# The seven-product feed-forward: p kept in the bank of h, new engine orders, a second tile in eight products, weight sums on VectorE

## The chip, the cores and the metric

One core of a Trainium2 chip runs the whole program. The metric is device time in microseconds (us) of one execution; lower is better. The kernel before takes 4196.09 us (median of 3 runs, 4193.67 to 4196.6).

## The reference, cut to what matters

Three stages follow each other on 24576 tokens of 256 numbers: a filter in the frequency domain, a mixture of experts, and a dense feed-forward. The change is in the last one alone:

```python
def _moe2_ref(x, w_in, w_out):      # x 3072*8 x 256, w_in 256 x 2048, w_out 2048 x 256
    h = x @ w_in
    g = h - np.tanh(h)
    return (g @ w_out).astype(np.float32)
```

The kernel is for small h. There g is h times a polynomial of third degree in u = h*h, written as g = (s + KAPPA) * p with p = c*h*u and s = (u + beta)^2.

## The kernel before

The first two stages fill the first 1776 us and are not touched. The feed-forward (`ff_phase`, line 1035) goes over 48 tiles of 512 tokens. The x of a tile (256 x 512) is cut into 2 x 2 blocks, and so is `w_in`; h of a tile then comes from seven block products in place of eight (Winograd's form of Strassen's scheme), with sums of the blocks of x and of the weights in place of the eighth. Every fp32 number is held as a high and a low part, so one block product M1 to M7 is three matmuls of 256 columns (`product`, line 1123). A tile has eight groups j; group g = 8*tile + j is 128 columns of each half of h, in two PSUM banks `B[0]` and `B[1]` (line 1061), with two pairs of banks that alternate between even and odd groups.

For each group the engines do this, by the names of the order tables:

- TensorE (PE): M5 and M1 into `B[0]`, then M6, M7, M2, M3, M4; and D0 to D7, the product with `w_out` of the group three before (`down`, line 1166): for each quarter of the tokens and each half f a matmul of 512 columns with the high part gh and one of 256 with the low part gl.
- ScalarE (ACT): `op1` copies half a bank of `B[0]` to `B[1]`, `opa` copies the other half to SBUF as A; `u0`, `u1` square the two banks; `s` squares again; `gh` rounds g to its high part.
- VectorE (DVE): `opb`, `opc` add A into the banks in place (line 1211); `p0`, `p1` make p from h and u, 128 x 512 each (line 1219); `g` makes (s + KAPPA) * p, 128 x 1024 in one instruction (line 1224).
- GpSimd (POOL): `gl` = g - gh, 128 x 1024 (line 1231).

Per tile there are also: the load of x and of the row numbers two tiles ahead (`ld`); four block subtractions on x (`ta` and `tb`, two each); their high parts on ScalarE (`ha`, `hb`, `hc`) and low parts on GpSimd (`la`, `lb`, `lc`); four sums of the finished output on VectorE (`sum0` to `sum3`, line 1173), and four indirect DMAs that scatter the rows to the output, issued by GpSimd (`row0` to `row3`, line 1177).

The order of work on each engine is written in two tables, `FIRST` for tile 0 and `LATER` for the others, one string for each group (lines 1005 to 1022). `SHIFT` says which group a name belongs to (D is three groups late, M5 and M1 one early), and `NEEDS` what must have been emitted before it. The engines run their lists in order and wait on each other by semaphores. Buffers set further waits: `p` has two buffers, so `p0` of a group waits for `gl` of the group two before; a bank of h is free for the group two later when `p0` and `p1` have read it.

Tile 0 is done in eight products (`plain`, line 1108: six matmuls of 512 columns for each half and group), since the sums of weight blocks `Sh` and `Sl` do not exist yet. They are made beside tile 0: `whole` adds high and low parts of `w_in` on GpSimd (line 1143), `sums_of` and `Sl` run on VectorE, `Sh` on ScalarE. Near the end `column_sums` (tile 45), `column_max` (tile 46) and `limit` (tile 47) work out a bound on h; a branch to a slow path behind it is not taken.

Of the kernel before, what the change touches and what calls it, by code (L numbers as in the profile page):

```python
# [988 lines left out]
def ff_first(tc, pool, x2T, ids, c):  # L989
# [43 lines left out]


def ff_phase(tc, x2T, ids, out, weights, mx, N, X0):
# [5 lines left out]
    with ExitStack() as es:  # L1041
# [89 lines left out]
        def sums_of(c):  # L1131
            w = slice(TH * c, TH * c + TH)
            v = nc.vector
            v.tensor_tensor(R[:, 0], F[:, 0, 1], F[:, 1, 1], op=ALU.add)
            v.tensor_tensor(R[:, 1], R[:, 0], F[:, 0, 0], op=ALU.subtract)
            v.tensor_tensor(R[:, 2], F[:, 0, 0], F[:, 0, 1], op=ALU.subtract)
            v.tensor_tensor(R[:, 3], F[:, 1, 0], R[:, 1], op=ALU.subtract)

        def whole(c):
            w = slice(TH * c, TH * c + TH)  # L1140
            a, b = [q.bitcast(F32).rearrange("p k (f n) -> p k f n", f=2) for q in (wih, wil)]
            for k in range(2):
                nc.gpsimd.tensor_tensor(F[:, k], a[:, k, :, w], b[:, k, :, w], op=ALU.add)  # L1143
# [42 lines left out]
        def emit(n, g):  # L1186
            t, j = divmod(g, 8)
            f = n[-1:].isdigit() and int(n[-1])
            if n[0] == "M":
# [22 lines left out]
            elif n[0] == "u":  # L1212
                if f == 0:
                    U[g] = tp.tile([128, 2, TM], F32, name="u")
                nc.scalar.activation(U[g][:, f], B[f][g % 2], AF.Square)  # L1215
            elif n[0] == "p":
                if f == 0:
                    Q[g] = tp.tile([128, 2, TM], F32, name="p")
                nc.vector.scalar_tensor_tensor(Q[g][:, f], B[f][g % 2], Q3[2], U[g][:, f], op0=ALU.mult, op1=ALU.mult)  # L1219
# [3 lines left out]
            elif n == "g":  # L1223
                nc.vector.scalar_tensor_tensor(Q[g], O.pop(g), KAPPA, Q[g], op0=ALU.add, op1=ALU.mult)  # L1224
                U.pop(g)
            elif n == "gh":
                G[g] = [tp.tile([128, 2, TM], F32R, name=n, bufs=3)]
                nc.scalar.activation(G[g][0], Q[g], AF.Copy)  # L1228
            elif n == "gl":
                G[g].append(tp.tile([128, 2, TM], F32R, name=n, bufs=3))  # L1230
                nc.gpsimd.tensor_tensor(G[g][1], Q.pop(g), G[g][0].bitcast(F32), op=ALU.subtract)  # L1231

        def extra(n, t):
            f = n[-1:].isdigit() and int(n[-1])
# [30 lines left out]
        def place(k, n):  # L1265
            t = k // 8
            if n in TILE:
                g = t + TILE[n]
                return (n, g) if 0 <= g < NT and (t or n[:2] not in ("su", "ro")) else None
            if n[0] in "FS":  # L1270
                return (n, 0) if t < 2 else None
            g = k + SHIFT.get(n, 0)
            return (n, g) if 0 <= g < NG and not (g < 8 and n in STEPS) else None
# [128 lines left out]
```

## Time and profile before

| | before |
|---|---|
| median of 3 runs | 4196.09 us |
| the profiled execution | 4197.41 us |
| its span in the trace | 4195.6 us |
| mean granted TensorE clock | 0.961 of full speed |
| PE busy, share of the span | 93% |
| VectorE, ScalarE, GpSimd busy | 68%, 61%, 59% |
| start of the feed-forward's first matmul | 1776.35 us |

The profiled execution is 1.3 us longer than the median, and 1.8 us of it lie outside the span. Busy time of PE overlaps: a matmul is shown to its modelled end, while the next one starts earlier, so the distance between starts tells the rate. All times below are us from the start of the span.

### The profile page before, as it was taken

The page shows a single profiled execution, that of the slowest core. Times are in us where ns is not written, and L with a number is a line of the kernel's source. Part 1 is how long each engine was busy: PE and PEld are TensorE (multiplying, and loading weights), DVE is VectorE, ACT ScalarE, POOL GpSimd, SP SyncE. Part 2 cuts the span into 40 slices and gives each one's busy share as a digit, 9 for nine tenths or more (in the row PEclk, how much of TensorE's full clock was granted, in tenths as well). Part 3 has the DMA queues.
Part 4 walks back from the last instruction along what each step waited for, and adds up shares of the span by engine and source line. Part 5 has one row for each costly group of instructions (what it writes and reads, how often), then busy time and mean ns, then how long its engine had stood idle before and what let it go on. Part 6 is the DMA issues. An engine that isn't in the chain of part 4 may idle for free.

```text
span 4195.6 us, 67878 instructions
## 1 busy us (share of the span) xinstructions
PE 3888.7 (93%) x23932; PEld 3499.4 (83%) x23932; DVE 2871.2 (68%) x4727; ACT 2556.9 (61%) x4396; POOL 2488.4 (59%) x1609
## 2 busy tenths in 40 slices
PE   6999899999999999979999998999999989999988
PEld 3666679999999999968888888888888888888877
DVE  4788866888888777666666656666666665666666
ACT  3666564555555555556666666666666666666665
POOL 2476664544444444466666666666666666666655
PEclk8999999999999999999999999999999999999999
DMA  8999863222332232100000000000000000000000
GB/s 260 285 293 292 252 174 105 62 80 77 79 79 57 76 77 70 53 16 21 21 26 21 22 25 21 21 21 21 21 26 21 26 21 21 21 21 21 26 16 16
DMA packets 296660, 300.39 MB, mean 72 GB/s; under 512 B 157041, under 2 KB 238970, under 8 KB 296314
## 3 DMA queue, kind: packets, MB, share of 16 engines
q1 hardware_dynamic: 233466, 191.28, 17.0%
q10 hardware_dynamic: 44416, 53.77, 3.9%
q0 software_dynamic: 18432, 50.95, 3.4%
q8 instruction: 190, 3.11, 0.3%
q14 instruction: 156, 1.28, 0.1%
HBM read 278.98 MB, written 132.24 MB: 98 GB/s over the span
## 4 chain that ended last, share of the span: by engine, by line
PE 31%; issue 11%; POOL 9%; DVE 5%; DMA 1%; ACT 1%; POOLq 0%; DVEq 0%
PE h L1129 16%; PE po L1168 10%; PE po L1169 5%; POOL out L1177 4%; POOL gl L1231 3%; POOL xl L1263 2%; DVE p L1224 2%; DVE h L1211 1%; DMA out<-ob,ix 1%; DVE ob L1173 1%; DVE p L1219 0%; ACT gh L1228 0%; POOL work L1143 0%; POOLq L1177 0%; ACT abs L1074 0%
## 5 line engine op out<-in xcount | busy, mean ns | idle before, releaser
L1231 POOL TENSOR_TENSOR gl<-p,gh 128x1024 fp32r<-128x1024 f32 x384 | 917.9, 2397 | 761.7 <-ACT gh L1228 586.8
L1168 PE MATMUL po<-wo,gh 128*128 128x512 f32 x3072 | 1156.3, 401 | 0.5 <-ACT gh L1228 0.5
L1169 PE MATMUL po<-wo,gl 128*128 128x256 f32 x3072 | 882.0, 287 | 136.6 <-POOL gl L1231 136.6
L1219 DVE SCALAR_TENSOR_TENSOR p<-h,u 128x512 f32<-128x512 f32 x768 | 525.3, 684 | 435.3 <-POOL gl L1231 250.2
L1215 ACT ACTIVATE u<-h 128x512 f32<-128x512 f32 x768 | 458.2, 597 | 513.0 <-PE h L1129 508.2
L1169 PEld LDWEIGHTS po<-wo,gl 128*128 128x128 f32 x3072 | 591.9, 193 | 153.6 <-POOL gl L1231 153.1
L1168 PEld LDWEIGHTS po<-wo,gh 128*128 128x128 f32 x3072 | 593.5, 193 | 75.0 <-ACT gh L1228 0.8
L1211 DVE TENSOR_TENSOR h<-h,A 128x256 f32<-128x256 f32 x752 | 322.8, 429 | 423.9 <-PE h L1129 407.7
L1224 DVE SCALAR_TENSOR_TENSOR p<-s,p 128x1024 f32<-128x1024 f32 x384 | 573.9, 1494 | 17.0 <-ACT s L1222 15.2
L822 POOL TENSOR_TENSOR w2l<-raw,w2h 128x1024 fp32r<-128x1024 f32 x126 | 339.2, 2693 | 392.5 <-ACT w2h L821 390.2
L1129 PE MATMUL h<-xh,Sh 128*128 128x256 f32 x1504 | 469.2, 312 | 78.0 <-DVE h L1211 71.7
L884 ACT ACTIVATE hh<-h 128x384 fp32r<-128x384 f32 (+1 forms) x548 | 266.4, 499 | 430.3 <-PE h L874 430.0
L1222 ACT ACTIVATE s<-u,beta 128x1024 f32<-128x1024 f32 x384 | 442.9, 1153 | 12.5
L1129 PEld LDWEIGHTS h<-xh,Sh 128*128 128x128 f32 x1504 | 301.2, 200 | 170.4 <-DVE h L1211 110.7
L1129 PE MATMUL h<-xl,Sh 128*128 128x256 f32 x1504 | 439.7, 292 | 0.0
L1129 PE MATMUL h<-xh,Sl 128*128 128x256 f32 x1504 | 439.1, 292 | 0.0
L1228 ACT ACTIVATE gh<-p 128x1024 fp32r<-128x1024 f32 x384 | 407.4, 1061 | 51.1 <-DVE p L1224 49.0
L874 PE MATMUL h<-yh,w1h 128*128 128x384 f32 (+1 forms) x1184 | 391.7, 331 | 14.9 <-DVE hl L885 11.2
L874 PE MATMUL h<-yh,w1l 128*128 128x384 f32 (+1 forms) x1184 | 387.7, 327 | 0.6 <-DVE w1l L822 0.5
L874 PE MATMUL h<-yl,w1h 128*128 128x384 f32 (+1 forms) x1184 | 387.4, 327 | 0.0
L902 PE MATMUL o<-hh,w2h 128*128 128x384 f32 (+1 forms) x1184 | 387.1, 327 | 0.0
L902 PE MATMUL o<-hh,w2l 128*128 128x384 f32 (+1 forms) x1184 | 387.0, 327 | 0.0
(243 smaller groups left out, 9062.2 us busy)
## 6 DMA issues: line engine op xcount, KB each, us to landing
raw<-in_w SPq DMA_DIRECT2D x256, 512.0 KB
y<-region SPq DMA_DIRECT2D x252, 99.0 KB
xt<-in_x SPq DMA_DIRECT2D x48, 512.0 KB
z1d<-a ACTq DMA_DIRECT2D x96, 256.0 KB
A<-z1d SPq DMA_DIRECT2D x64, 384.0 KB
z3d<-b ACTq DMA_DIRECT2D x128, 192.0 KB
bt<-z3d SPq DMA_DIRECT2D x96, 256.0 KB
x2T<-x SPq DMA_DIRECT2D x63, 384.0 KB
```

Of the source, the lines that this page charges most:

```text
L874: nc.tensor.matmul(h[j], p[:, k, c], q[:, k], start=n == 0, stop=n == 5)
L902: nc.tensor.matmul(O[v][d], p[:, fb, c], q[:, j], start=fb == 0 and n == 0 and (d == 0 or v >= KV), stop=fb == 7 and n == 2 and (d == 1 or ...
L1129: nc.tensor.matmul(h, a[:, w], b, start=n == "M5" and a is ah and b is xh, stop=False, skip_group_check=True)
L1168: nc.tensor.matmul(po, gh[:, c], flat(wo[:, f]), start=begin, stop=False)
L1169: nc.tensor.matmul(po[:, :D], gl[:, c], wo[:, f, 0], start=False, stop=end)
L1211: nc.vector.tensor_tensor(B[n == "opc"][g % 2][:, first], B[1][g % 2][:, second], A5[g % 2], op=ALU.add)
L1215: nc.scalar.activation(U[g][:, f], B[f][g % 2], AF.Square)
L1219: nc.vector.scalar_tensor_tensor(Q[g][:, f], B[f][g % 2], Q3[2], U[g][:, f], op0=ALU.mult, op1=ALU.mult)
L1222: nc.scalar.activation(O[g], U[g], AF.Square, bias=beta)
L1224: nc.vector.scalar_tensor_tensor(Q[g], O.pop(g), KAPPA, Q[g], op0=ALU.add, op1=ALU.mult)
L1228: nc.scalar.activation(G[g][0], Q[g], AF.Copy)
L1231: nc.gpsimd.tensor_tensor(G[g][1], Q.pop(g), G[g][0].bitcast(F32), op=ALU.subtract)
```

## The change

- **p in the bank.** `p0` and `p1` write over h in its own PSUM bank. `g` is split in `g0` and `g1`, 128 x 512 each, which read s from SBUF and p from the bank. The two-buffer tile `p` is gone; g has two buffers of its own, needed only from `g0` on. A bank is now free for the group two later when `g0` (first bank) and `g1` (second bank) are done, where it was free after `p0` and `p1`.
- **New orders.** The tables `FIRST`, `SECOND` and `LATER` hold one list for a whole tile. The scatters stand apart and late, the four subtractions on x are single names `t1` to `t4`.
- **Two tiles in eight products.** `CLASSIC = 2`: tiles 0 and 1 use `plain`; tile 1's blocks of x get their parts by `cx` (ScalarE) and `cl` (GpSimd).
- **Weight sums on VectorE.** The adds of `whole` move from GpSimd (eight of 128 x 512) to VectorE (four of 128 x 1024), and the sums are spread over tiles 0 and 1.
- `column_sums` is emitted behind `s` of four groups of tile 45, and `limit` behind `g1` of the second group of tile 47.

```diff
 FIRST = dict(
...
+SECOND = dict(
...
 LATER = dict(
...
-    POOL=("ta gl", "tb gl", "la gl", "gl row0 row1 row2 row3 lb", "lc gl ld", "gl", "gl", "gl"),
+    POOL=("gl gl t3 t1 t2 gl la gl t4 gl gl lc lb ld gl row2 gl row1 row0 row3"),
 )
...
+    M5=("lb", "g0-2"), M1=("M5", "la"), M6=("op1", "lb"), M7=("opb", "lc"), M3=("opb", "la"), M2=("opb", "opa", "la", "g0-2"), M4=("opc", "lc", "g1-2"),
...
+CLASSIC = 2
...
-                if t:
+                if t >= CLASSIC:
...
             elif n[0] == "u":
-                if f == 0:
+                if g not in U:
                     U[g] = tp.tile([128, 2, TM], F32, name="u")
                 nc.scalar.activation(U[g][:, f], B[f][g % 2], AF.Square)
             elif n[0] == "p":
-                if f == 0:
-                    Q[g] = tp.tile([128, 2, TM], F32, name="p")
-                nc.vector.scalar_tensor_tensor(Q[g][:, f], B[f][g % 2], Q3[2], U[g][:, f], op0=ALU.mult, op1=ALU.mult)
+                h = B[f][g % 2]
+                nc.vector.scalar_tensor_tensor(h, h, Q3[2], U[g][:, f], op0=ALU.mult, op1=ALU.mult)
             elif n == "s":
                 O[g] = tp.tile([128, 2, TM], F32, name="s", bufs=1)
                 nc.scalar.activation(O[g], U[g], AF.Square, bias=beta)
-            elif n == "g":
-                nc.vector.scalar_tensor_tensor(Q[g], O.pop(g), KAPPA, Q[g], op0=ALU.add, op1=ALU.mult)
-                U.pop(g)
+                U.pop(g - 1, None)
+                if t == NT - 3 and j > 3:
+                    column_sums(j - 4)
+            elif n in ("g0", "g1"):
+                if f == 0:
+                    Q[g] = tp.tile([128, 2, TM], F32, name="g")
+                nc.vector.scalar_tensor_tensor(Q[g][:, f], O[g][:, f], KAPPA, B[f][g % 2], op0=ALU.add, op1=ALU.mult)
+                if (t, n, j) == (NT - 1, "g1", 1):
+                    limit()
...
             elif n[0] == "F":
-                whole(f)
+                a, b = [q.bitcast(F32).rearrange("p k (f n) -> p k f n", f=2) for q in (wih, wil)]
+                nc.vector.tensor_tensor(F, a[:, :, :, c], b[:, :, :, c], op=ALU.add)
...
```

The order of instructions shows what the tables do. First, GpSimd over one steady tile before: x<-x are the subtractions, xl the low parts, out the row scatters.

```order
L1251 TENSOR_TENSOR x<-x 128x256
L1252 TENSOR_TENSOR x<-x 128x256
L1231 TENSOR_TENSOR gl<-p,gh 128x1024
L1254 TENSOR_TENSOR x<-x 128x256
L1255 TENSOR_TENSOR x<-x 128x256
L1231 TENSOR_TENSOR gl<-p,gh 128x1024
L1263 TENSOR_TENSOR xl<-x,xh 128x768
L1231 TENSOR_TENSOR gl<-p,gh 128x1024 x2
L1177 DMA out<-ob,ix 24576x256 x4
L1263 TENSOR_TENSOR xl<-x,xh 128x512 x2
L1231 TENSOR_TENSOR gl<-p,gh 128x1024 x4
```

And the same engine over one steady tile of the changed kernel:

```order
L1237 TENSOR_TENSOR gl<-g,gh 128x1024 x2
L1264 TENSOR_TENSOR x<-x 128x256 x3
L1237 TENSOR_TENSOR gl<-g,gh 128x1024
L1275 TENSOR_TENSOR xl<-x,xh 128x768
L1237 TENSOR_TENSOR gl<-g,gh 128x1024
L1264 TENSOR_TENSOR x<-x 128x256
L1237 TENSOR_TENSOR gl<-g,gh 128x1024 x2
L1275 TENSOR_TENSOR xl<-x,xh 128x512 x2
L1237 TENSOR_TENSOR gl<-g,gh 128x1024
L1178 DMA out<-ob,ix 24576x256
L1237 TENSOR_TENSOR gl<-g,gh 128x1024
L1178 DMA out<-ob,ix 24576x256 x3
```

The four scatters and two low parts that stood in one run between the third and the fourth gl are now three runs: two low parts, one scatter, three scatters.

Second, VectorE where group 1 of a steady tile ends and group 2 begins, before. h_20430 and h_20432 are the two banks of even groups, h_20431 and h_20433 those of odd ones.

```order
L1219 SCALAR_TENSOR_TENSOR p<-h_20431,u 128x512
L1211 TENSOR_TENSOR h_20430<-h_20432,A_25157 128x256
L1219 SCALAR_TENSOR_TENSOR p<-h_20433,u 128x512
L1211 TENSOR_TENSOR h_20432<-h_20432,A_25157 128x256
L1173 TENSOR_REDUCE ob<-po 128x256
L1224 SCALAR_TENSOR_TENSOR p<-s,p 128x1024
```

And in the changed kernel:

```order
L1219 SCALAR_TENSOR_TENSOR h_20431<-h_20431,u 128x512
L1212 TENSOR_TENSOR h_20430<-h_20432,A_24506 128x256
L1219 SCALAR_TENSOR_TENSOR h_20433<-h_20433,u 128x512
L1212 TENSOR_TENSOR h_20432<-h_20432,A_24506 128x256
L1229 SCALAR_TENSOR_TENSOR g<-s,h_20431 128x512
L1229 SCALAR_TENSOR_TENSOR g<-s,h_20433 128x512
L1174 TENSOR_REDUCE ob<-po 128x256
```

p goes back to the banks h_20431 and h_20433, the two halves of g read them there, and the output sum stands behind g.

Third, VectorE in tile 45, where the column sums are added (l<-abs,abs), before:

```order
L1219 SCALAR_TENSOR_TENSOR p<-h_20431,u 128x512
L1075 TENSOR_TENSOR l_20437<-abs_42011,abs_42012 128x512
L1211 TENSOR_TENSOR h_20430<-h_20432,A_41978 128x256
L1219 SCALAR_TENSOR_TENSOR p<-h_20433,u 128x512
L1211 TENSOR_TENSOR h_20432<-h_20432,A_41978 128x256
```

And in the changed kernel:

```order
L1229 SCALAR_TENSOR_TENSOR g<-s,h_20433 128x512
L1090 TENSOR_TENSOR l_20437<-abs_42287,abs_42288 128x512
L1219 SCALAR_TENSOR_TENSOR h_20432<-h_20432,u 128x512
L1219 SCALAR_TENSOR_TENSOR h_20430<-h_20430,u 128x512
L1212 TENSOR_TENSOR h_20431<-h_20433,A_42283 128x256
```

In both, the add stands ahead of the add into a bank (opb) that the next block products wait for.

## Rows read from the trace of the kernel before

**Rows 1.** Windows: stretch, us, busy of PE PEld DVE ACT POOL, PEclk, DMA, GB/s
```profile
1776.00:1830.00 54.00, 40.48 (x185) 32.02 (x184) 37.46 (x40) 29.21 (x39) 34.26 (x21) 0.97 0.10 27
1830.00:1886.00 56.00, 47.75 (x297) 43.08 (x296) 36.08 (x49) 33.85 (x55) 35.30 (x21) 0.90 0.07 19
1886.00:4017.00 2131.00, 1958.83 (x12734) 1783.49 (x12733) 1310.71 (x1892) 1397.92 (x2194) 1423.61 (x818) 0.95 0.08 22
4017.00:4079.00 62.00, 50.19 (x301) 45.42 (x300) 38.65 (x50) 37.03 (x61) 35.31 (x22) 0.89 0.06 18
4079.00:4177.00 98.00, 88.44 (x593) 79.39 (x592) 69.92 (x108) 63.24 (x98) 53.75 (x30) 1.00 0.03 12
```

**Rows 2.** Timeline of PE without waits: start, duration, engine, line, operation
```profile
2802.34 0.39 PE L1168 MATMUL po<-wo,gh 128*128 128x512 f32 x1
...
2803.39 0.28 PE L1129 MATMUL h<-xh,Sh 128*128 128x256 f32 x1
...
2805.15 0.40 PE L1168 MATMUL po<-wo,gh 128*128 128x512 f32 x1
```

**Rows 3.** Timeline of PE, same tile, at D0 of group 3
```profile
2812.97 0.40 PE L1168 MATMUL po<-wo,gh 128*128 128x512 f32 x1
2816.29 0.39 PE L1169 MATMUL po<-wo,gl 128*128 128x256 f32 x1 [2.92 <-POOL gl L1231]
...
2818.16 0.41 PE L1129 MATMUL h<-xh,wih 128*128 128x256 f32 x1
...
2820.48 0.28 PE L1129 MATMUL h<-xh,Sl 128*128 128x256 f32 x1
```

**Rows 4.** Timeline of POOL, same tile, from gl of group 2 on
```profile
2802.51 2.40 POOL L1231 TENSOR_TENSOR gl<-p,gh 128x1024 fp32r<-128x1024 f32 x1 [3.24 <-issue]
2805.07 2.00 POOL L1177 DMA_INDIRECT out<-ob,ix  x1 [0.16 <-issue]
...
2811.37 2.57 POOL L1263 TENSOR_TENSOR xl<-x,xh 128x512 fp32r<-128x512 f32 x2
2813.86 4.69 POOL L1231 TENSOR_TENSOR gl<-p,gh 128x1024 fp32r<-128x1024 f32 x2
```

**Rows 5.** Waits, tiles 2 to 44: who for whom, us in total, times, longest
```profile
DVE p L1219 <- POOL gl L1231: 241.2, 42, 5.8
...
PE po L1169 <- POOL gl L1231: 123.6, 43, 2.9
...
PE h L1129 <- DVE h L1211: 48.6, 129, 1.6
```

**Rows 6.** Groups of instructions, tiles 2 to 44: busy us, mean ns of one
```profile
L1231 POOL TENSOR_TENSOR gl<-p,gh 128x1024 fp32r<-128x1024 f32 x345 | 823.5, 2393 | 659.6 <-ACT gh L1228 505.0 <-issue 140.9 <-PE h L1129 13.7
...
L1224 DVE SCALAR_TENSOR_TENSOR p<-s,p 128x1024 f32<-128x1024 f32 x344 | 513.4, 1492 | 12.2 <-ACT s L1222 10.5
L1219 DVE SCALAR_TENSOR_TENSOR p<-h,u 128x512 f32<-128x512 f32 x688 | 470.8, 684 | 401.1 <-POOL gl L1231 241.2 <-ACT u L1215 158.5
...
L1215 ACT ACTIVATE u<-h 128x512 f32<-128x512 f32 x689 | 411.3, 597 | 467.2 <-PE h L1129 462.9
...
L1222 ACT ACTIVATE s<-u,beta 128x1024 f32<-128x1024 f32 x344 | 396.8, 1153 | 11.2
L1228 ACT ACTIVATE gh<-p 128x1024 fp32r<-128x1024 f32 x344 | 364.9, 1061 | 37.1 <-DVE p L1224 35.1
...
L1211 DVE TENSOR_TENSOR h<-h,A 128x256 f32<-128x256 f32 x688 | 295.4, 429 | 394.9 <-PE h L1129 379.8 <-ACT u L1215 2.3 <-issue 0.3
```

**Rows 7.** Timeline of VectorE and POOL, one g beside one xl
```profile
2842.42 2.14 DVE L1224 SCALAR_TENSOR_TENSOR p<-s,p 128x1024 f32<-128x1024 f32 x1
...
2841.64 1.84 POOL L1263 TENSOR_TENSOR xl<-x,xh 128x768 fp32r<-128x768 f32 x1
```

**Rows 8.** Lines 1224 and 1075: ns min/median/max of one instruction
```profile
L1224 DVE SCALAR_TENSOR_TENSOR p<-s,p x384: 1207/1216/6597, 1781.1 to 4177.3; 128x1024 f32<-128x1024 f32 x192
...
L1075 DVE TENSOR_TENSOR l<-abs,abs x4: 1910/1968/3493, 4040.2 to 4069.5; 128x512 fp32r<-128x512 f32 x4
```

More of the change, by code (lines that the diff above doesn't have):

```diff
@@ L1022 @@
+    POOL=("gl gl t3 t1 t2 gl la gl t4 gl gl lc lb ld gl row2 gl row1 row0 row3"),
 )
 STEPS = ("M1", "M3", "M5", "M6", "M7", "op1", "opa", "opb", "opc")
-TILE = dict(ta=1, tb=1, ha=1, hb=1, hc=1, la=1, lb=1, lc=1, ld=2, **{f"{n}{i}": -1 for n in ("sum", "row") for i in range(4)})
-SHIFT = dict(**{f"D{i}": -3 for i in range(8)}, M5=1, M1=1, op1=1, opa=1, u1=-1, s=-1, p1=-1, g=-1, gh=-1, gl=-1)
+TILE = dict(**{n: 1 for n in "t1 t2 t3 t4 ha hb hc la lb lc cx cl".split()}, ld=2, **{f"{n}{i}": -1 for n in ("sum", "row") for i in range(4)})
@@ L1026 @@
+SHIFT = dict(**{f"D{i}": -3 for i in range(8)}, M5=1, M1=1, op1=1, opa=1, u1=-1, s=-1, p1=-1, g0=-1, g1=-1, gh=-1, gl=-1)
 NEEDS = dict(
-    M5=("lb", "p0-2"), M1=("M5", "la", "p0-2"), M6=("op1", "lb"), M7=("opb", "lc"), M3=("opb", "la"), M2=("opb", "opa", "la"), M4=("opc", "M7", "lc", "p1-2"),
-    op1=("M1", "p1-2"), opa=("M1", "opb-2", "opc-2"), opb=("M6", "opa"), opc=("M7", "opa"), u0=("M2", "M3", "p1-2", "s-2"), u1=("M4", "u0"),
-    s=("u0", "u1", "g-1"), p0=("u0", "gl-2", "gh-2"), p1=("u1", "p0"), g=("s", "p0", "p1"), gh=("g", "D7-3"), gl=("gh", "D7-3"),
@@ new lines @@
+    op1=("M1", "g1-2"), opa=("M1", "opb-2", "opc-2"), opb=("M6", "opa"), opc=("M7", "opb"), u0=("M2", "M3", "p1-2", "s-2"), u1=("M4", "p1-2", "s-2"),
+    s=("u0", "u1", "g0-1", "g1-1"), p0=("u0",), p1=("u1",), g0=("s", "p0", "gl-2"), g1=("p1", "g0"), gh=("g0", "g1", "D7-3"), gl=("gh", "D7-3"),
+    **{f"D{i}": ("gl",) for i in range(8)}, **{f"row{i}": (f"sum{i}",) for i in range(4)},
+    **{f"{n}{i}": (f"{m}{i}",) for n, m in (("Sa", "F"), ("Sb", "Sa"), ("Sh", "Sb"), ("Sl", "Sh")) for i in range(4)},
@@ L1035, in ff_phase @@
+    **{f"F{i}": (f"Sb{i - 1}",) for i in range(1, 4)},
+    t1=("ld",), t2=("t1",), t3=("ld",), t4=("t2", "t3"), ha=("ld",), hb=("t1", "t2"), hc=("t3", "t4"), la=("ha",), lb=("hb",), lc=("hc",),
+    cx=("ld",), cl=("cx",))
+CLASSIC = 2
 def ff_phase(tc, x2T, ids, out, weights, mx, N, X0):
@@ L1129, in product @@
                 nc.tensor.matmul(h, a[:, w], b, start=n == "M5" and a is ah and b is xh, stop=False, skip_group_check=True)
[L1131 to L1143, printed above, removed]
         def general(h):
@@ L1263, in extra @@
                     nc.gpsimd.tensor_tensor(xl, v, xh.bitcast(F32), op=ALU.subtract)
[L1265 to L1273, printed above, removed]
+        once = lambda n: n in TILE or n[0] in "FS"
+        exists = lambda n, g: 0 <= g < (NT if n in TILE else NG) and not (g < 8 * CLASSIC and n in STEPS)
         def ready(n, g):
```

95 lines of the change are left out of this document (53 added, 42 removed), and 6 rows, old and new, of the table PE.

## The prediction

> **What bounds the kernel now.** I read the windows by stretch first: tile 0 to 1830, tile 1 to 1886, tiles 2 to 44 to 4017, tile 45 to 4079, tiles 46 and 47 to 4177. Tiles 2 to 44 take 2131 us and hold 12734 matmuls of PE [rows 1]. A tile issues 8 x (7 x 3 + 8 x 2) = 296 matmuls, so the stretch is 43.0 tiles of 49.5 us. No engine is full there: VectorE 1311, ScalarE 1398, GpSimd 1424 of 2131 us, and the clock is 0.95 on average.
>
> The timeline of PE says what a tile would take without waits. From 2802.34 to 2803.39 lie three D steps, 0.35 us each; from there to 2805.15 fifteen matmuls of 256 columns, 0.1173 us each [rows 2]. One product is then 0.352 us, a group 7 x 0.352 + 8 x 0.35 = 5.26 us, a tile 42.1 us. So 7.4 us of each tile are lost, 320 us over 43 tiles. Nearly all the stake of this change is there.
>
> Where they are lost is one place. At D0 of group 3 PE waits for gl [rows 3], 43 times in 43 tiles, 123.6 us in all, 2.9 us each [rows 5]. Behind it the clock is at its lower level, 1.2 GHz: a matmul shown with 0.28 us elsewhere has 0.41 at 2818.16, and 0.28 again at 2820.48 [rows 2, 3]. In tiles 46 and 47, where the clock reads 1.00 throughout [rows 1], nothing of this remains. From 2812.97 to 2820.48 PE issues what costs 2.0 us undisturbed (two D steps and eleven matmuls); it took 7.5, so 5.5 of the 7.4 us hang on this wait. The other 1.9 us are short waits for VectorE's adds into the banks (129 waits, 48.6 us as PE shows them [rows 5]) and the rest of the slow stretch.
>
> Why gl is late is in GpSimd's timeline [rows 4]. Behind gl of group 2 come four scatters and two xl, from 2805.07 to 2813.86, 8.8 us in one run (the scatters 6.3, so 1.58 each with the gap behind it). Only then gl of group 3 starts. The wait goes back further: p has two buffers, so VectorE's p0 stood up to 5.8 us behind gl, 42 times [rows 5], and with it all that follows in VectorE's list.
>
> **The change, part by part.**
>
> *The scatters.* The longest run of foreign work between two gl is now three scatters, 3 x 1.58 = 4.7 us, then two xl (2.57) and three subtractions. From the end of M4 of a group to the end of its gl the rows give u 0.60, s 1.15, two halves of g 1.37, gh 1.06, gl 2.39 [rows 6], together 6.6, with five handoffs of 0.1 to 0.2 us (0.16 between two GpSimd instructions [rows 4]) 7.2 us. In the new PE order 33 to 39 steps lie between M4 of a group and its D0, 11.6 to 13.7 us. So a gl may stand 4.4 us behind other work on the average place, and the three scatters stand at group 7, which has 12.6 us and bears 5.4. Before, 8.8 us stood against 4.4 at group 3: 4.4 us too late by this count, about 4 in the trace (2.9 of idle and a step that ends late). I walked once through a steady tile this way, each engine's new list against PE's unhindered steps: gl is done 0.6 to 1.5 us before its D in all eight groups, closest at groups 1 and 2, where ScalarE's list puts gh behind the next u1 and s. So the 5.5 us per tile go.
>
> *The bank held longer.* M5 of a group now waits for g0 of the group two before, where it waited for p0. From the end of M4 to g0's end lie u 0.60, s 1.15, g0 0.68 and handoffs, 2.9 us; PE has 10 to 14 steps there, 3.5 to 4.9 us. It fits, with 0.35 us to spare at the two closest places (M5 of groups 3 and 5, where VectorE's list puts opc ahead of g0). op1, which refills the second bank, waits for g1 and has 0.6 us or more. What is late next if this is misjudged is M5, and behind it op1, M6 and the whole group.
>
> *p in place, g in halves.* No row shows 128 x 512 written back to PSUM. Nearest are opc and opb, which write 128 x 256 into a bank, 0.429, and p from PSUM to SBUF, 0.684 [rows 6]. The step from 256 to 512 elements is about 0.26 us, the same as from 512 (0.684) to the uncontended 1024 (1.216 [rows 8]) for each 256. So writing to a bank or to SBUF shows the same fixed part, and I take 0.68, with 0.65 to 0.9 as bounds (twice 0.429 above). Two halves of g cost 1.37 for 1.22 alone, but the mean of g now is 1.492 [rows 6]. VectorE gets about 1 us per tile lighter, in its idle time: worth nothing by itself.
>
> Why g's mean is above its least: in one place g starts at 2842.42 while an xl runs to 2843.48, and takes 2.14, 0.93 over its least, about the time it had to wait [rows 7]. The Trainium skill (SBUF — State Buffer, section Who interferes with whom) says that a VectorE instruction with two SBUF inputs and a GpSimd instruction that reads SBUF shut each other out, whoever comes second waiting for the other's end, and that one with at most one SBUF input does not contend. The trace agrees for g, 2.14 against 1.21. By the rule g0 and g1, with s in SBUF and p in PSUM, never wait for GpSimd; without it they would keep up to 0.93 us now and then, which is a rival below.
>
> *Short waits at the adds.* In the new order M6 and M7 are at least three steps apart (1.04 us), before in places one (0.35), while opb with its handoffs needs about 0.8 (0.429 plus handoffs). Most of the 1.9 us go. I leave 0.4 us per tile for what the walk does not see: 42.5 us, so 43 x (49.5 - 42.5) = 301 us gained.
>
> *Tiles 0 and 1.* Tile 0 took 54 us [rows 1]. Its work is 16 halves of six 512-column matmuls (0.35 - 0.117 = 0.233 each, 22.4 us) and 40 D steps (14.0), 36.4 us. GpSimd's weight sums stood ahead of gl there; they leave GpSimd. I take 39, with 2.6 us to fill the pipe: 15 gained. Tile 1 took 56; in eight products its work is 22.4 + 64 x 0.35 + 0.7 = 45.5, that is 3.4 us more than in seven. I take 46.5: 9.5 gained. The adds on VectorE (two of 1024 and two Sl of 1024 per tile at 1.22, eight small ones at 0.43) add 8.3 us to 16 x 1.37 = 21.9 of p and g. By waits for GpSimd they could each grow by a gl, 2.4, to 40 us per tile in all, still under 45. So they hide behind PE; if that cover failed, it is 5 to 10 us once.
>
> *Tiles 45 to 47.* Tile 45 took 62, 12.5 over the others, since four adds of 1.9 to 3.5 us [rows 8] stand ahead of opb. They still do, so I keep 12.5: 55, 7 gained. Tiles 46 and 47 took 98 against 84.2 unhindered; half of that loss is work (column maximum, bound on h) that stays: 91, 7 gained.
>
> *The end.* The last scatters now begin with row2, two output sums later than row0. A sum reads as many elements as a p, 0.68 [rows 6]: 1.4 us lost.
>
> **The sum.** The profiled execution is 4197.4 us (span 4195.6). 4197.4 - 301 - 15 - 9.5 - 7 - 7 + 1.4 = 3859.3. The median of the runs is 1.3 below the profiled one, so 3858 us. About 0.2% is what a measurement of this kernel can tell from no change.
>
> **The rivals.**
>
> *Part of the wait stays* (24%). GpSimd (1424 of 2131 us busy, two thirds, and more in a shorter tile: 33 of 42) and ScalarE run close to full, and the walk leaves only 0.6 us at two places. If gl still comes 1 to 2 us late once a tile, that is 43 x 2 = 86 us, 3944. If it comes 3 us late and the clock falls again, 5 us a tile, 215 us, 4073. Contention that lasts belongs here: 0.93 us on g0 at the two or three closest places is 2 us a tile, 3944 again. The page named above rules out this last case. For the rival: the scatters varied (one took 2.00 [rows 4]). Against it: the runs of foreign work are half as long, and p0 no longer waits for gl.
>
> *The banks become the bound: slower* (6%). M5 waits for g0 in every group. Over eight groups PE has 33.6 us between M4 and M5. If M4 to g0 took c, the tile would lose 8c - 33.6; it is slower than before from a loss of 7.4, c = 5.1 us, against my 2.9. That needs VectorE to reach g0 2.2 us late in every group, as when an opc ahead of it waits for an M7 that is itself late. At c = 5.5 the tile is 52.5, and the time 4290. For it: g0 stands behind opc in its list, and every engine waits in order. Against it: each link has its price in rows, and the sum is short of 5.1 by nearly half.
>
> *The search changes nothing in steady tiles* (2%). Then only the first and last tiles count, 38 us, 4160; within 0.2% of before only if these fail too.
>
> **How the numbers follow.** The forecast, PE unhindered but for less than 1 us a tile, gets 68%; its own range is 3835 (tile at 42.1, first tiles 6 us better) to 3901 (tile at 43.5). The range must hold 80%: half of the first rival is added, up to 3 us a tile, 3858 + 129 = 3987. The lower end is near what PE's own work allows. So 3830 to 3990. Faster 0.92, same 0.02, slower 0.06.
>
> **What would show it.** A steady tile of 42 to 43 us in the windows by stretch, clock 1.00 there in place of 0.95; no wait of PE for gl at group 3; no wait of p0 for gl; g0 and g1 at 0.68 each with hardly any spread, p at 0.68 to 0.70; gl at 2.4. Tile 0 near 39 and tile 1 near 46. Wrong would be: PE waiting for ScalarE or VectorE ahead of M5 or M6 in every group, p in place well over 0.9, or GpSimd still ending last before a D.

## The result, and the profile after

The changed kernel takes 3860.8 us (median of 4 runs, 3860.3 to 3860.9), the kernel before 4196.4 in the same measurement: ratio 0.920, 95% interval 0.9185 to 0.9217. The forecast was 3858. The profiled execution has a span of 3858.8 us in place of 4195.6.

The windows by stretch of the changed kernel, with its own tile starts as bounds: tile 0, tile 1, tile 2, tiles 3 to 44, tile 45, tiles 46 and 47, and what follows. The columns are those of [rows 1].

```profile
1774.17:1816.00 41.83, 38.77 (x177) 31.29 (x177) 31.67 (x43) 25.93 (x35) 16.95 (x8) 0.96 0.13 35
1816.00:1866.49 50.49, 47.60 (x232) 39.40 (x231) 37.47 (x48) 30.97 (x40) 28.08 (x16) 0.97 0.04 11
1866.49:1914.70 48.21, 45.25 (x298) 42.06 (x297) 32.86 (x53) 33.99 (x54) 31.95 (x21) 0.93 0.07 23
1914.70:3688.50 1773.80, 1773.80 (x12435) 1658.49 (x12433) 1220.06 (x2184) 1377.62 (x2143) 1276.22 (x799) 1.00 0.09 26
3688.50:3741.92 53.42, 46.09 (x298) 42.21 (x297) 30.74 (x55) 36.20 (x58) 32.97 (x21) 0.94 0.08 23
3741.92:3834.36 92.44, 86.77 (x593) 78.91 (x591) 63.99 (x125) 64.06 (x100) 50.57 (x30) 1.00 0.03 11
3834.36:3858.80 24.44, 10.35 (x50) 8.50 (x48) 4.19 (x7) 1.65 (x2) 11.73 (x10) 0.75 0.13 45
```

From tile 3 to tile 44 PE is busy for the whole of 1773.80 us, 42.23 a tile, at full clock: nothing is left there but PE's own 42.1. Tiles 2 to 44 took 2131 us and take 1822, so 309 of the 337 us come from there. Tile 0 gave 12, tile 1 5.5, tile 45 8.6, tiles 46 and 47 5.6; the feed-forward starts 1.8 us ahead of the 1776 from which [rows 1] counts it, and the end behind tile 47 lost 5.8 (18.6 before, from 4177 to the end of the span).

The groups of instructions of tiles 3 to 44 (busy us, mean ns), which answer to [rows 6]:

```profile
L1237 POOL TENSOR_TENSOR gl<-g,gh 128x1024 fp32r<-128x1024 f32 x337 | 812.6, 2411 | 455.2 <-ACT gh L1234 348.6 <-DVE g L1229 105.3
...
L1219 DVE SCALAR_TENSOR_TENSOR h<-h,u 128x512 f32<-128x512 f32 x672 | 461.7, 693 | 82.8 <-ACT u L1216 82.7
L1229 DVE SCALAR_TENSOR_TENSOR g<-s,h 128x512 f32<-128x512 f32 x672 | 436.7, 681 | 6.8
...
L1178 POOL DMA_INDIRECT out<-ob,ix x168 | 165.9, 988 | 39.1 <-issue 26.4 <-PE h L1144 12.7
```

p in place costs 0.693 us (0.684 to SBUF before), half a g 0.681, so a whole g 1.36 in place of a mean of 1.492. p waits for u alone; its 241 us of waiting for gl [rows 5, 6] are gone.

From the end of M4 to M5 two groups on PE's list leaves 3.34 to 3.36 us ahead of M5 of groups 2, 3 and 5, and 4.0 to 4.8 at the others. One of these three closest places, M4 of group 1 to M5 of group 3, in one steady tile: timelines of PE (M4's last matmul, M5's first), ScalarE and VectorE.

```profile
2810.97 0.28 PE L1144 MATMUL h<-xh,wil 128*128 128x256 f32 x1
...
2814.61 0.28 PE L1144 MATMUL h<-xh,Sh 128*128 128x256 f32 x1
...
2811.29 0.60 ACT L1216 ACTIVATE u<-h 128x512 f32<-128x512 f32 x1
2811.92 1.15 ACT L1222 ACTIVATE s<-u,beta 128x1024 f32<-128x1024 f32 x1
2812.98 1.04 ACT L1234 ACTIVATE gh<-g 128x1024 fp32r<-128x1024 f32 x1
...
2813.07 0.43 DVE L1212 TENSOR_TENSOR h<-h,A 128x256 f32<-128x256 f32 x1 [0.31 <-PE h L1144]
2813.41 1.27 DVE L1229 SCALAR_TENSOR_TENSOR g<-s,h 128x512 f32<-128x512 f32 x2
```

M4 ends at 2811.25, g0 (the first 0.68 of the 1.27) at 2814.1: 2.85 us, and M5 starts 0.5 later without a wait. gh of the group before stands behind u and s.

GpSimd and PE in the same tile at group 2, where gl has the least time:

```profile
2825.00 2.41 POOL L1237 TENSOR_TENSOR gl<-g,gh 128x1024 fp32r<-128x1024 f32 x1 [1.90 <-ACT gh L1234]
...
2828.32 0.39 PE L1169 MATMUL po<-wo,gh 128*128 128x512 f32 x1
```

gl ends at 2827.41, 0.9 us ahead of its D0.

### The profile page after: what moved, and what is told of

It reads as the page before. It is cut to its first block, busy times and chain, and to the rows that moved or that the text cites. A ratio compares the mean times of both kernels' runs of the same rounds, so it can differ in the third digit from the quotient of the medians.

```text
span 3858.8 us, 67578 instructions
## 1 busy us (share of the span) xinstructions
PE 3742.3 (97%) x23860; PEld 3410.2 (88%) x23860; DVE 2797.6 (73%) x5099; ACT 2564.7 (66%) x4378; POOL 2351.8 (61%) x1595
## 3 DMA queue, kind: packets, MB, share of 16 engines
q14 instruction: 155, 1.27, 0.1%
## 4 chain that ended last, share of the span: by engine, by line
PE 77%; DVE 3%; ACT 1%; DMA 1%; issue 1%; POOL 0%; ACTq 0%; SPq 0%; POOLq 0%; DVEq 0%
PE h L1144 24%; PE po L1169 17%; PE h L874 13%; PE o L902 13%; PE po L1170 9%; DVE g L1229 1%; DMA out<-ob,ix 0%; DMA raw<-in_w 0%; DMA region<-Y,pi 0%; ACT gh L1234 0%; ACT s L1222 0%; DVE hl L885 0%; DVE h L1219 0%; ACT u L1216 0%; DVE yl L853 0%
## 5 line engine op out<-in xcount | busy, mean ns | idle before, releaser
L1237 POOL TENSOR_TENSOR gl<-g,gh 128x1024 fp32r<-128x1024 f32 x384 | 925.4, 2410 | 594.4 <-ACT gh L1234 442.9
L1170 PE MATMUL po<-wo,gl 128*128 128x256 f32 x3072 | 864.8, 282 | 3.6 <-POOL gl L1237 3.6
L1169 PEld LDWEIGHTS po<-wo,gh 128*128 128x128 f32 x3072 | 582.1, 189 | 73.0 <-DVE ob L1174 3.7
L1219 DVE SCALAR_TENSOR_TENSOR h<-h,u 128x512 f32<-128x512 f32 x768 | 527.8, 693 | 106.2 <-ACT u L1216 106.1
L1229 DVE SCALAR_TENSOR_TENSOR g<-s,h 128x512 f32<-128x512 f32 x768 | 498.7, 681 | 9.9 <-ACT s L1222 2.2
L1144 PE MATMUL h<-xh,Sh 128*128 128x256 f32 x1472 | 415.0, 282 | 15.2 <-DVE h L1212 11.8
L1234 ACT ACTIVATE gh<-g 128x1024 fp32r<-128x1024 f32 x384 | 403.4, 1051 | 30.6 <-DVE g L1229 30.6
L1144 PE MATMUL h<-xh,Sl 128*128 128x256 f32 x1472 | 413.6, 281 | 0.0
L1144 PE MATMUL h<-xl,Sh 128*128 128x256 f32 x1472 | 413.5, 281 | 0.0
L902 PE MATMUL o<-hl,w2h 128*128 128x384 f32 (+1 forms) x1184 | 387.2, 327 | 0.0
```

What stands on the lines that cost most here:

```text
L902: nc.tensor.matmul(O[v][d], p[:, fb, c], q[:, j], start=fb == 0 and n == 0 and (d == 0 or v >= KV), stop=fb == 7 and n == 2 and (d == 1 or ...
L1144: nc.tensor.matmul(h, a[:, w], b, start=n == "M5" and a is ah and b is xh, stop=False, skip_group_check=True)
L1169: nc.tensor.matmul(po, gh[:, c], flat(wo[:, f]), start=begin, stop=False)
L1170: nc.tensor.matmul(po[:, :D], gl[:, c], wo[:, f, 0], start=False, stop=end)
L1219: nc.vector.scalar_tensor_tensor(h, h, Q3[2], U[g][:, f], op0=ALU.mult, op1=ALU.mult)
L1229: nc.vector.scalar_tensor_tensor(Q[g][:, f], O[g][:, f], KAPPA, B[f][g % 2], op0=ALU.add, op1=ALU.mult)
```

## The experiments

Eleven kernels, all against the kernel before, which took 4197.6 to 4198.7 us beside them and 4196.4 beside the changed kernel: a difference of 2 or 3 us between two of them shows nothing by itself. The time of one steady tile is read from the profiled execution, between the starts of tiles 3 and 44. The first, third and fourth kernel leave out three of the last tile's four scatters, a few us of work.

| kernel | median us | ratio, 95% interval | steady tile us |
|---|---|---|---|
| before, scatters apart | 3952.2 | 0.9394 to 0.9425 | 44.0 |
| before, third p buffer | 4149.0 | 0.986 to 0.9893 | 48.4 |
| scatters apart, p in the bank, old order | 4239.4 | 1.0081 to 1.0112 | 50.3 |
| the same, gh one group later | 4114.7 | 0.9787 to 0.982 | 47.8 |
| changed, scatters in a run | 3967.6 | 0.9432 to 0.9463 | 44.7 |
| changed, p in SBUF | 3973.8 | 0.9445 to 0.9476 | 44.5 |
| changed, gh ahead at three groups | 3878.7 | 0.9224 to 0.9254 | 42.6 |
| changed, Sl on GpSimd | 3855.4 | 0.9172 to 0.9197 | 42.2 |
| changed, column sums on PE | 3847.1 | 0.9152 to 0.9177 | 42.2 |
| one tile in eight products | 3862.0 | 0.9185 to 0.921 | 42.2 |
| all together | 3830.4 | 0.911 to 0.9134 | 42.2 |

**The scatters alone.** In the kernel before, `POOL` of `LATER`. The run stands between the fourth and the fifth gl of a tile, those of groups 2 and 3 (not the third and the fourth, as the section on the change has it).

```diff
-    POOL=("ta gl", "tb gl", "la gl", "gl row0 row1 row2 row3 lb", "lc gl ld", "gl", "gl", "gl"),
+    POOL=("ta gl", "tb gl", "la gl", "gl lb", "lc gl ld row0", "gl row1", "gl row2", "gl row3"),
```

> The kernel before, with only its four scatters set apart: one behind gl in each of the last four groups of a tile in place of four in a run ahead of gl of group 3. Theory (the order of the work on GpSimd is the cause): the run ahead of gl of group 3 falls from 8.8 us to one xl of 1.3 us, so PE's wait for gl at D0 of group 3 goes and the clock stays at 2.4 GHz: 5.5 us per tile gained, 43 x 5.5 = 237, about 3960 us. Rival (p in the bank and the shorter VectorE work are the cause): hardly a gain, 4150 us or more, with the wait at another group.

3952.2 us, 8 below the theory's 3960: 246 of the 336 us from one line. A few us of that are the scatters left out; 43 steady tiles with 5.5 us each are 237. Window, wait and groups of its tiles 3 to 43:

```profile
1927.87:3733.01 1805.14, 1773.08 (x12139) 1618.89 (x12137) 1327.11 (x1804) 1338.20 (x2092) 1464.74 (x780) 1.00 0.08 25
...
PE h L1129 <- DVE h L1211: 32.1, 123, 0.6
...
L1224 DVE SCALAR_TENSOR_TENSOR p<-s,p 128x1024 f32<-128x1024 f32 x328 | 568.0, 1732 | 19.2 <-ACT s L1222 19.2
...
L1177 POOL DMA_INDIRECT out<-ob,ix x164 | 260.5, 1588 | 27.3 <-issue 15.4 <-PE h L1129 6.6
```

The wait for gl is gone and the clock is 1.00. A tile still takes 1.9 us more than PE's own 42.1, and the only wait that PE shows is for the adds, 123 times, three in each tile, 0.8 us a tile. The rival, that p in the bank does it, falls for this part.

**A third buffer for p alone.** `Q[g]` gets `bufs=3`, and `p0` needs `gl-3`.

> The kernel before, with a third buffer for p and nothing else moved (the room comes from two small tiles of tile 45 that use the free sums' room instead). p0 then waits for gl of the group three before, which takes VectorE off GpSimd as p in the bank does. Theory (the scatters' place is the cause): the run of 8.8 us still stands ahead of gl of group 3, which can bear 4.4, so the wait at D0 of group 3 stays and the gain is 1 us per tile at most: 4150 to 4196 us. Rival (the p buffers held VectorE up and that made gl late): the wait falls by more than half, 4060 us or less.

4149.0: 50 us, 1 us more than the theory gave at most, and far from the rival's 4060. p0's wait for gl disappears, PE's does not:

```profile
1940.62:3923.94 1983.32, 1842.59 (x12138) 1684.78 (x12137) 1236.98 (x1804) 1330.49 (x2092) 1368.30 (x780) 0.96 0.08 23
...
PE po L1169 <- POOL gl L1231: 119.7, 41, 3.0
```

So the 5.8 us for which p0 stood behind gl [rows 5] are worth 1 us a tile. They were a consequence of the run of scatters: with the scatters apart no wait of p for gl is left either.

**The run put back in the changed kernel.**

```diff
-    POOL=("gl gl t3 t1 t2 gl la gl t4 gl gl lc lb ld gl row2 gl row1 row0 row3"),
+    POOL=("gl gl t3 t1 t2 gl la gl t4 row0 row1 row2 row3 lb gl gl lc ld gl gl"),
```

> The changed kernel, with one piece of GpSimd's list put back near its old place: one subtraction, the four scatters and lb in one run ahead of gl of group 3; p stays in the bank. Theory (order): the run costs 0.74 + 4 x 1.2 + 1.28 = 6.8 us, where the place bears 12.3 - 7.2 = 5.1; gl is 1.7 us late in each tile, PE waits as long at D0 of group 3 and the clock falls behind it: 2 to 5 us per tile, 3945 to 4075 us. Rival (p in the bank alone makes the late run harmless, since VectorE no longer waits for gl): within 0.5% of the changed kernel, 3861 to 3880 us.

3967.6, 107 us lost, within the theory's range: the wait is back, so p in the bank does not make a late gl harmless. GpSimd and PE in one tile, and the window behind the wait:

```profile
2885.70 0.75 POOL L1264 TENSOR_TENSOR x<-x 128x256 f32<-128x256 f32 x1
...
2892.72 4.72 POOL L1237 TENSOR_TENSOR gl<-g,gh 128x1024 fp32r<-128x1024 f32 x2
...
2895.14 0.38 PE L1170 MATMUL po<-wo,gl 128*128 128x256 f32 x1 [2.09 <-POOL gl L1237]
...
2895.20:2899.00 3.80, 3.80 (x26) 3.54 (x27) 2.60 (x4) 2.16 (x5) 3.48 (x2) 1.00 0.00 0
```

The run, one subtraction, four scatters and one xl, is 7.0 us, PE stands 2.1 (1.7 expected from the budget), and the clock behind it stays 1.00 here, against the expectation; over tiles 3 to 43 it is 1.00 too.

**p in SBUF again, all else as changed.** p gets one tile for each half; g0 and g1 read it there. Two small tiles of the column sums give up their room for it.

> The changed kernel with all its new orders, but p written to SBUF (one buffer for each half) in place of the bank of h; g0 and g1 read s and p from SBUF, two SBUF inputs. The banks are still held to g by the written order alone. Theory (order is the cause, and the bank of h only takes the contention away): g0 and g1 grow from 0.68 to somewhat more beside GpSimd's work, up to 1.6 now and then, and a scatter goes from 0.99 back to 1.3 us; a tile loses 0 to 2 us: 3861 to 3947 us. Rival (p in the bank is most of the gain): 4050 us or more.

3973.8, 27 us above the theory's range and 76 below the rival's. Its window, its groups and PE's one wait, tiles 3 to 43:

```profile
1928.95:3752.01 1823.06, 1754.14 (x12138) 1617.76 (x12137) 1444.93 (x2132) 1349.23 (x2092) 1398.82 (x780) 1.00 0.08 25
...
L1239 POOL TENSOR_TENSOR gl<-g,gh 128x1024 fp32r<-128x1024 f32 x328 | 847.3, 2583 | 382.7 <-ACT gh L1236 321.8 <-DVE g L1231 59.9
L1231 DVE SCALAR_TENSOR_TENSOR g<-s,p 128x512 f32<-128x512 f32 x656 | 698.1, 1094 | 6.9 <-issue 0.3 <-DVE h L1212 0.2
...
PE h L1144 <- DVE h L1212: 68.9, 85, 1.2
```

Half a g now takes 1.094 us in place of 0.681: 16 x 0.413 = 6.6 us of VectorE's time per tile, and gl grows by 0.17. VectorE is late with the adds, and PE waits for it twice a tile, 1.7 us as PE shows it; a tile loses 2.2 us, which is 94 of the 113 us over 42 tiles. A scatter takes 1.05, not the 1.3 expected. The Trainium skill (SBUF — State Buffer, Who interferes with whom) has it so: two SBUF inputs contend with GpSimd's reads, one does not; the trace agrees, 1.094 against 0.681.

**p in the bank, old order.** The kernel with the scatters apart; p over h, g in two halves ahead of opc in VectorE's list.

> The kernel before with its scatters set apart (as in the first run) and with p in the bank of h and g in two halves of 128 x 512, in the old order of work; only VectorE's list has g ahead of opc, without which the lists would wait on each other. Three of the last tile's four scatters are left out, as in the first run. Theory (p in the bank needs the new orders, since M5 now waits for g0): in the old order of PE the distance from the end of M4 to M5 two groups on is 1.75 us once, 2.45 twice, 3.15 to 5.2 else, and M4 to g0 takes 2.9 to 3.1 us, so a tile loses 1.2 + 0.6 + 0.6 = 2 to 3 us more than with the scatters apart alone: 4000 to 4075 us, with waits of M5 for g. Rival (p in the bank is a gain by itself, since VectorE no longer stands beside GpSimd): 3950 us or less.

4239.4, 1% slower than before, and far outside the theory's range too. The window and PE's wait in tiles 3 to 43, then one M5 of group 3 and the window behind it:

```profile
1934.88:3998.77 2063.89, 1881.00 (x12139) 1671.13 (x12137) 1197.38 (x2132) 1327.30 (x2092) 1241.54 (x780) 0.98 0.07 22
...
PE h L1129 <- DVE g L1226: 159.4, 211, 1.9
...
2802.48 1.05 ACT L1230 ACTIVATE gh<-g 128x1024 fp32r<-128x1024 f32 x1
2803.42 0.60 ACT L1215 ACTIVATE u<-h 128x512 f32<-128x512 f32 x1
2804.05 1.15 ACT L1221 ACTIVATE s<-u,beta 128x1024 f32<-128x1024 f32 x1
...
2804.31 0.43 DVE L1211 TENSOR_TENSOR h<-h,A 128x256 f32<-128x256 f32 x1 [1.56 <-PE h L1129]
2804.65 0.69 DVE L1218 SCALAR_TENSOR_TENSOR h<-h,u 128x512 f32<-128x512 f32 x1
2805.29 1.28 DVE L1226 SCALAR_TENSOR_TENSOR g<-s,h 128x512 f32<-128x512 f32 x2
...
2806.04 0.38 PE L1129 MATMUL h<-xh,Sh 128*128 128x256 f32 x1 [1.82 <-DVE g L1226]
...
2806.30:2809.80 3.50, 3.50 (x17) 3.31 (x17) 1.40 (x3) 0.00 (x0) 1.47 (x1) 0.54 0.25 57
```

Two chains end together at 2805.2 to 2805.3. On ScalarE u stands 1.0 us behind gh of the group before. On VectorE opb needs M6, which PE issues directly ahead of M5, and opb, p1 and g0 take 1.7 us one after the other. PE waits for g in five or six of eight groups, 3.9 us a tile in all, and behind the longest of these waits the clock is near its lower level, 0.54.

**gh one group later in that kernel** (`gh=-2, gl=-2` in `SHIFT`, gh behind s in each group).

> As the run with p in the bank in the old order (three of the last tile's four scatters left out again), with one thing more: gh, and gl with it, stands one group later in ScalarE's and GpSimd's lists, behind u1 and s of the next group in place of ahead of them. In that run's trace u1 stood 1.0 us behind gh, and M4 to M5 took 3.6 us where the chain alone is 2.9. Theory (gh ahead of u1 makes the bank come free late): the chain falls to 2.9, PE waits only where M4 to M5 is 1.75 and 2.45: 45 to 48 us per tile, 3990 to 4110 us. Rival (VectorE's list or the old order of PE alone is what costs it): 4180 us or more.

4114.7: 125 us back, 5 us above the range's end. PE still waits for g in tiles 3 to 43:

```profile
PE h L1129 <- DVE g L1226: 88.4, 123, 1.8
```

Up to 1.8 us of it, most of the 2.2 a tile, lie between M6 and M5 of group 3, the chain opb, p1, g0. So gh ahead of u is not quite half of the 287 us that p in the bank costs here against the scatters apart alone. Of the 3.8 us a tile that are left, PE's waits for g are 2.2, and the mean clock of 0.97 over these tiles is worth up to 1.4 (0.03 of 47.8), an estimate. That M6 next to M5 in PE's list makes the wait is read from the trace; no run moved them apart.

**gh ahead at three groups of the changed kernel.**

```diff
-    ACT=("u1 s ha u0 op1 opa u1 s gh u0 op1 opa u1 s gh u0 op1 opa u1 s gh u0 hb op1 opa u1 s gh u1 u0 op1 opa"
+    ACT=("u1 s ha u0 op1 opa gh u1 s u0 op1 opa gh u1 s u0 op1 opa gh u1 s u0 hb op1 opa u1 s gh u1 u0 op1 opa"
```

> The changed kernel with gh back ahead of the next u1 and s on ScalarE at three of eight groups (gh of the group before the tile and of groups 0 and 1), nothing else moved. Theory (the bank in the new order hangs on gh standing behind u1 and s): M4 to g0 grows by up to 1.0 us at three places where M5 has 0.4 to 0.7 to spare, so PE waits for g0 there, 1 to 3 us per tile: 3900 to 3990 us. Rival (the place of gh does not matter, since ScalarE is a third idle): 3861 to 3870 us.

3878.7: a miss for both. A tile loses 0.4 us, where the theory had 1 to 3 and the rival nothing; PE's weight loads wait for g by 0.2 us at most (10.9 us in all). In the new order gh's place at these three groups decides little.

**Sl on GpSimd.** At the start of tile 2 of the changed kernel Sl spans a whole gl of GpSimd, and opb, M7 and PE stand behind it (VectorE, GpSimd, PE):

```profile
1866.68 3.94 DVE L1259 TENSOR_TENSOR Sl<-work,Sh 128x1024 fp32r<-128x1024 f32 x1 [2.10 <-ACT Sh L1257]
...
1867.15 2.38 POOL L1237 TENSOR_TENSOR gl<-g,gh 128x1024 fp32r<-128x1024 f32 x1
...
1871.02 0.58 PE L1144 MATMUL h<-xh,Sh 128*128 128x256 f32 x1 [2.96 <-DVE h L1212]
```

The edit takes `Sl0` to `Sl3` out of VectorE's lists, puts them into GpSimd's and writes `nc.gpsimd` at their line.

> The changed kernel with the four Sl (low parts of the weight sums, 128 x 1024, two SBUF inputs) on GpSimd in place of VectorE. Theory (the first tiles are late since these wait on VectorE for GpSimd's work, 2.1 to 3.9 us each, the last one ahead of opb at the start of tile 2): the wait of 3.1 us at the start of tile 2 goes and the 1.2 GHz stretch behind it, 4 to 6 us, and 1 to 3 us in tiles 0 and 1: 3852 to 3856 us. Rival (tile 2 is late since the pipe of seven products has to fill there): 3859 us or more, the wait at M7 of tile 2's first group still there.

3855.4, in the range. The five runs reach from 3850.7 to 3860.1, so the total alone is not clear of the changed kernel's 3860.8; the tiles tell it. Tile 2 takes 42.61 in place of 48.21 us and tile 0 38.56 in place of 41.83; tile 1 does not gain (51.74). Windows of tiles 0 to 2:

```profile
1775.16:1813.72 38.56, 36.88 (x177) 30.11 (x177) 28.55 (x41) 24.66 (x33) 20.34 (x8) 1.00 0.14 38
1813.72:1865.46 51.74, 47.93 (x233) 39.42 (x231) 33.59 (x48) 31.77 (x41) 32.67 (x18) 0.97 0.04 11
1865.46:1908.07 42.61, 42.53 (x299) 39.48 (x297) 29.20 (x52) 34.10 (x54) 33.65 (x22) 1.00 0.08 26
```

**Column sums on PE.**

```diff
-            nc.vector.tensor_tensor(l1[:, c], *a, op=ALU.add)
...
-            nc.tensor.matmul(t, ones, l1[:, TM * q : TM * q + TM], start=True, stop=True)
+            for k in range(2):
+                nc.tensor.matmul(t, ones, l1[:, q % 2, k], start=k == 0, stop=k == 1)
```

> The changed kernel with the column sums of the bound on h made on PE: ScalarE writes the absolute values of both halves of the rows, and PE adds them up in two matmuls of 512 columns in place of one, so VectorE's four adds of 128 x 512 in tile 45 go. Two of the four pairs of absolute values move from tile 45 to tile 46. Theory (the four adds, 1.9 to 3.5 us each ahead of VectorE's other work, cost tile 45 its 11 us): tile 45 takes 43 to 45 us in place of 53.4, four more matmuls cost 0.9: 3850 to 3854 us. Rival (ScalarE's eight absolute values are what makes the tile late): 3857 us or more.

3847.1, 14 us less and 3 below the theory's range; tile 45 falls from 53.42 to 42.23 us. The reason given was only half right: the four adds of the changed kernel take 0.693 each, not 1.9 to 3.5 (one line's view: their duration, and what VectorE stood for ahead of them), but VectorE stood 15.3 us for ScalarE's absolute values before them. The edit also moves two of the four pairs of absolute values to tile 46, so the run does not tell whether the adds' wait on VectorE or the load of ScalarE made the tile late.

```profile
3689.14:3731.37 42.23, 42.23 (x299) 39.50 (x298) 28.94 (x52) 33.68 (x54) 30.42 (x20) 1.00 0.09 26
...
L1090 DVE TENSOR_TENSOR l<-abs,abs x4: 693/693/693, 3716.4 to 3743.4; 128x512 fp32r<-128x512 f32 x4
...
  ACT abs L1089: 15.3, 4
```

**One tile in eight products, Sl on GpSimd.**

> As the run with Sl on GpSimd, but tile 0 alone in eight products: all four weight sums beside tile 0, tile 1 in seven products with the order of the later tiles. Theory (a second tile in eight products buys time for the sums): beside one tile the sums do not fit; VectorE has 21.9 us of p and g, 4.9 of F and sixteen small adds of 0.41 to 1.6, 34 to 52 us against 36.4 of PE's work, and M5 and M1 of the next tile need the first chunk. Tile 0 grows from 42 to 46 to 50 us, tile 1 falls from 50 to 44: the two together within 3 us of the run with Sl on GpSimd. Rival (the second tile in eight products is only PE work, 3.4 us of it): 3 to 8 us faster than that run.

3862.0, 6.6 above the run with Sl on GpSimd: a miss for both. Tile 1 falls to 42.22 us, but tile 0 takes 58.25, not 46 to 50, and the two together take 10.2 us more than in that run. With this order the second tile in eight products buys time for the sums; whether a better order of tile 0 would do without it was not tried.

**All together.** Besides the two edits above: `FIRST` and `SECOND` written anew (F2 at the end of tile 0, sum2 and sum3 ahead of g, lb ahead of lc), the column maximum in `B[1]`, and a table for the last tile:

```diff
+LAST = dict(LATER, POOL="gl gl gl gl gl row0 row1 gl row2 row3 gl gl")
```

> The changed kernel with the parts that helped put together and four more edits outside the steady tiles: Sl on GpSimd and the column sums on PE as in the two runs before; the weight sums of tile 1 begun at the end of tile 0 and the output sums of tile 0 taken earlier, since PE waits 2.5 and 1.1 us for them in tile 1; the column maximum in the second bank, where M5 does not wait for it; in the last tile the scatters of the tile before ahead of gl of group 4, not ahead of the last gl, and its own scatters in the order of their sums. Theory (what is left above PE's own work lies in the first and the last tiles and hangs on single waits): tile 0 39 us, tile 1 48, tile 2 43, tile 45 42, tile 46 45, 3 to 5 us at the end: 3825 to 3838 us. Rival (the first and last tiles are bound by filling and draining the pipe): 3842 us or more, which is what the two edits gave one by one.

3830.4, in the theory's range and 30 us below the changed kernel. Tiles 0, 1, 45, 46 with 47, and the end:

```profile
1783.02:1821.62 38.60, 36.89 (x178) 30.10 (x178) 27.64 (x39) 25.21 (x34) 20.57 (x9) 1.00 0.14 38
1821.62:1867.18 45.56, 45.56 (x233) 38.29 (x232) 34.54 (x49) 32.01 (x42) 36.64 (x20) 1.00 0.07 18
...
3683.59:3726.01 42.42, 42.42 (x299) 39.51 (x297) 28.95 (x52) 33.69 (x54) 30.41 (x20) 1.00 0.09 26
3726.01:3814.94 88.93, 86.94 (x596) 79.83 (x595) 63.59 (x124) 66.03 (x104) 57.48 (x35) 1.00 0.06 19
3814.94:3833.80 18.86, 8.56 (x50) 7.27 (x48) 4.18 (x7) 1.65 (x2) 7.62 (x6) 0.80 0.09 31
```

In tiles 0, 1 and 45 PE's waits are gone but for 1.7 us in tile 0; so they were single waits, not the filling of the pipe. Which of the edits took which away is not separated. The feed-forward starts between 1774 and 1784 us in these profiles, whatever its own code, so parts of a few us are compared by tiles.

## Why the prediction was right, and where it was not

**The scatters: right.** The forecast put 5.5 of 7.4 us on the run ahead of gl of group 3. Taking it apart in the old kernel gives 49.5 - 44.0 = 5.5; putting it back in the new one costs 2.5. The walk's spare for gl is there too, and larger: the forecast had 0.6 to 1.5 us in the eight groups, closest at groups 1 and 2; in the trace gl is done 0.9 us (group 2) to 3.8 us (group 4) ahead of its D0.

**The bank: right in size.** M4 to g0 takes 2.85 us (2.9 forecast), with 0.5 to spare (0.35). The rival that ends slower is real: in the old order the bank makes 4239. Its condition was stated as a chain of 5.1 us from M4 in every group; what decides in the trace is 3.6 us at one place, M4 of group 1 to M5 of group 3, where PE takes 1.6 in the kernel with the scatters apart, and a chain that starts at M6, over opb and p1.

**"VectorE gets about 1 us per tile lighter, in its idle time: worth nothing by itself": the step that failed.** The forecast let the new order alone take the 1.9 us of short waits. With the scatters apart these are the runs:

| steady tile us | p in SBUF | p in the bank |
|---|---|---|
| old order | 44.0 | 50.3 |
| new order | 44.5 | 42.2 |

The new order with p in SBUF gains nothing over the old one, and the bank in the old order loses 6.3. Only both together give the last 2 us, since VectorE's halves of g are then 0.681 us and not 1.094. The four kernels differ in a little more than rows and columns say: in the first g is one instruction of 128 x 1024, in the second VectorE's list has g ahead of opc. The longer g is what grew in the trace with p in SBUF; the forecast had weighed that case (its rival's 0.93 us on g0, 2 us a tile), but gave p in the bank no term in the sum. It is worth 113 us. The sum stayed right, because the change has both.

**The terms, mis-sized.** A steady tile came to 42.2 where 42.5 was taken; tiles 2 to 44 are 1822 against 1830 (2131 - 301), although tile 2 alone took 48.2. Tile 0 took 41.8 (39), tile 1 50.5 (46.5), tile 45 53.4 (55), tiles 46 and 47 92.4 (91), the end 5.8 (1.4). The forecast said of the weight sums that "they hide behind PE": they did not, since Sl takes up to 3.9 us beside GpSimd's work and stands ahead of p1 or opb, shown by the run with Sl on GpSimd: tile 0 gets 3.3 us and tile 2 5.6, within the 5 to 10 that the forecast named for that case. In tile 1 PE waits 2.9 us for output sums that VectorE comes to late; these waits went in the last run, with other edits. The end is late since three scatters stand ahead of the last gl: PE's D0 of the last group waits 2.7 us for it, and does not in the last run. The steady tiles came out 8 us shorter than the sum had them and the rest 9 longer; the misses nearly cancel, and that 3858 came within 3 us is partly luck.

**Still open:** the new orders were tested as a whole, so which engine's list gives p in the bank its room is not separated, beyond gh's place at three groups; no run tried M6 and M5 apart in the old order; and the loss of 0.4 us with gh ahead was not followed further.

## What to carry to other kernels

Look for the longest run of foreign work ahead of a due instruction on an engine that works in order, and compare it with the time that the place has; one line of a table was worth 246 us here. A buffer kept longer and an order of work are one change: test each alone and both, because either alone may lose. On VectorE beside a busy GpSimd, count the instructions with two SBUF inputs, also those that run once: a single one of 128 x 1024, a size for which the adds of `whole` (F) take 1.2 us, became 3.9 and cost tile 2 5.6.

## What was not expected of the hardware

PE stood 2.09 us for gl in the run with the scatters put back, and the granted clock behind it is 1.00. It stood 2.92 in the kernel before [rows 3], and the matmuls behind it take 0.41 us in place of 0.28, the level of 1.2 GHz. So the same kind of wait costs a tile 2.5 us in one kernel, little more than its own length, and 5.5 in the other. The length of the wait does not order them: in the old order with p in the bank PE stood 1.82 us, less than 2.09, with another 0.84 some 5.6 us earlier, and the clock behind it is 0.54. What decides is not shown here.

The issue of a scatter on GpSimd takes 0.988 us with g's input in the bank, 1.052 to 1.588 us in the mean with two SBUF inputs beside it. The clearest pair is the old order with the scatters apart, where GpSimd's list is the same: 1.588 with p in SBUF, 0.993 with p in the bank. GpSimd is held up by VectorE as well, not only the other way.
